# First batch in two parts of 256 and 320 queries, two buffers of turned P, one of x, and tile 1's scores beside P V

## The chip, the cores and the metric

The kernel runs on one core of a Trainium2 chip. A core has five engines that run side by side: TensorE (PE, matmuls, with its weight loads shown as PEld), VectorE (DVE), ScalarE (ACT), GpSimd (POOL) and SyncE (SP, which here only issues DMAs). Each engine takes its instructions strictly in the order in which they were written and waits at an instruction until its operands are there. The metric is the time of one execution on the device in microseconds (us); lower is better.

## The reference

Block-causal attention over 8 batches of 8 heads, 576 positions of 64 values each, followed by a feed-forward layer with three first matrices whose maximum is taken:

```python
# q, k, v: (8, 8, 576, 64) float32;  w1, w2, w3: (512, 768), w_out: (768, 512) float64
scores = scale * np.matmul(q, k.transpose(0, 1, 3, 2))
mask = block_i >= block_j                    # blocks of 64 positions
scores = np.where(mask, scores, -1000000000.0)
attn = np.exp(scores - np.max(scores, axis=-1, keepdims=True))
attn = attn / (np.sum(attn, axis=-1, keepdims=True) + 1e-09)
attn_out = np.matmul(attn, v)                # -> x: 4608 tokens of 512
h = np.maximum(np.maximum(x @ w1, x @ w2), x @ w3)
out = h @ w_out
```

## The kernel before

**Attention.** Two heads are a pair; a batch has four pairs, the program 32. Queries are cut into tiles of 128: tile t (0 to 3) needs the first 128(t+1) keys, and the last 64 queries of both heads make a tile 4 of their own over all 576 keys. A pair goes through these steps: load q, k and v (`load`, DMAs issued by SP); turn k and q on DVE (`turn_k`, `turn_q`, tile `kq`); scores on PE (`qk` in the groups (3,), (2,) and (1, 0), and `qk4`), into PSUM banks `sb`; scan for the maximum with the mask on DVE (`top`, `top4`, line 382); exponential on ACT (`exp`, line 445); sum and inverse on DVE; scale by the inverse on ACT or POOL (`scale`); turn P in 32 x 32 blocks on DVE into `pz` (`turn`, lines 470 and 474); move `pz` to `pt` by four DMAs for each head (`move`, line 480); and P V on PE (`pv`, line 651). The two halves of the result, 256 and 320 columns wide, are copied from PSUM to `x32`, and split into a high and a low part `xh`, `xl` (`out`, `x_high`, `x_low`).

**Weights.** The weights come as 64-bit numbers. A unit (class `Unit`, 24 of them: 18 of w1, w2, w3 and 6 of w_out) loads 512 KB and makes a high and a low part of it: `size` on ACT, five steps on DVE (`clamp`, `shift`, `sign`, `power`, `rest`), `high` on ACT, three matmuls on PE (`whole`, lines 325 to 327), `lower` on ACT. All 24 stand near the start of the program.

**Feed-forward.** A `Chunk` is one half (320 or 256 columns) of a batch: 18 products on PE (`product`, line 764, 12 matmuls each), the maximum on DVE (`most`, line 779), a high and a low part of h on ACT and POOL, and the projection (`project`, line 830). A chunk needs its half of all four pairs of its batch, and its weights.

**Order.** The code makes a list of jobs, each with costs by engine, a rank, the jobs that it follows and the buffers that it takes and gives. `in_order` plays the list through and writes down, engine by engine, the order in which the jobs begin; the program holds that order fixed. `rank` grows by `PAIR` for each pair; units get ranks `DELAY + PACE * u`. The numbers of buffers are in `slots`: one of `pz`, three of `x32`, one natural copy of q and k each.

Of the kernel before, what the change touches and what calls it, by code (L numbers as in the profile page):

```python
# [19 lines left out]
INF = 3.0e38  # L20
# [121 lines left out]
def kernel(  # L142
# [23 lines left out]
    DELAY = 60.0  # L166
    PACE = 3.0

    PAIR = 24
    TURN = 12  # L170
    NEAR = 2
    XB = 3
# [4 lines left out]
        x32_0=XB, x32_1=XB, xh0=4, xl0=4, xh1=4, xl1=4, m=2, osb=2, left=1, qn=1, kn=1,  # L177
        vn=2, kq=2, q8=2, pz=1, pt=3, rest=1,
# [59 lines left out]
    class Unit:  # L238


        def __init__(self, u, src, dst, n, prior, *early):
# [16 lines left out]
            for step, fast in (  # L258
                (self.clamp, True),
                (self.shift, True),  # L260
                (self.sign, False),
                (self.power, True),
                (self.rest, False),
            ):
                c = dve(512, fast)
                j = job({"DVE": c}, rank, step, after=(j,), take=("rest",) if step == self.rest else (), lasts=c + GAP)
            j = job({"ACT": act(512, False)}, rank, self.high, after=(j,))
            j = job({"PE": 6 * pe(512)}, rank, self.whole, after=(j,), take=("pm",), give=(*self.temps, "rest"))
# [47 lines left out]
        def rest(self, eng):  # L316
            self.c = moe.tile([P, 512], F32R, name="rest", bufs=1)
# [59 lines left out]
    )  # L377

    GROUPS = ((3,), (2,), (1, 0))
# [15 lines left out]
    class Head:  # L395
# [5 lines left out]
        def plan(self, t0):  # L401

            pair, exps = self.pair, {}
            for n, ts in enumerate(GROUPS):
                apart = None
                for t in ts:
# [3 lines left out]
                        t0 + n + 1,  # L410
# [3 lines left out]
                        take=("stat",) if n == 0 else (),  # L414
# [3 lines left out]
                    exps[t] = job({"ACT": act(m) + 185.0}, t0 + n + 2, self.exp, t, after=(d,), take=(f"p{t}",))  # L418
                join([exps[t] for t in ts], BANK)
            inv = job({"DVE": SMALL}, t0 + 5, self.sum, after=exps.values(), lasts=SMALL + GAP)  # L420
            inv = job({"DVE": SMALL}, t0 + 5, self.inverse, after=(inv,))
            scales = {
                t: job(norm_cost(P * (t + 1)), t0 + 7 + t / 2, self.scale, t, after=(inv,)) for t in range(4)
            }
            join(scales.values(), ("stat",))
            first = job({"DVE": dve(512) + dve(128)}, t0 + 11, self.turn, 4, after=(pair.scaled,), take=("pz",))
            self.turned = [first]
            for t in (3, 2, 1, 0):
                j = job({"DVE": dve(P * (t + 1))}, t0 + 12, self.turn, t, after=(scales[t], first))
                join((j,), (f"p{t}",))  # L430
                self.turned.append(j)
            self.moved = job(
                {"SP": 4 * SEND}, t0 + 13, self.move, after=self.turned, take=("pt",), give=("pz",), lasts=4 * SEND + TURNED
            )

        def top(self, eng, t):
# [3 lines left out]
            least(self.ps[t], mask[:, 512 - P * (t + 1) :], INF, self.stat[0][:, t : t + 1])  # L440

        def exp(self, eng, t):
            nm, sm, _ = self.stat
            self.p[t] = att.tile([P, P * (t + 1)], F32, name=f"p{t}", bufs=slots[f"p{t}"])
            nc.scalar.activation(  # L445
                self.p[t], self.ps.pop(t), AF.Exp, bias=nm[:, t : t + 1], scale=-1.0, accum_out=sm[:, t : t + 1]
            )

        def sum(self, eng):
            nc.vector.tensor_scalar_add(self.stat[2], self.stat[1], EPS)  # L450

        def inverse(self, eng):
            nc.vector.reciprocal(self.stat[2], self.stat[2])  # L453

        def scale(self, eng, t):
            normalise(eng, self.p[t], self.stat[2][:, t : t + 1])

        def turn(self, eng, t):

            if t == 4:  # L460
                self.pz = att.tile([P, 4 * (RUN + 16)], F32, name="pz", bufs=slots["pz"])
# [14 lines left out]
        def move(self, eng):  # L476
            self.pt = att.tile([P, 4, RUN], F32, name="pt", bufs=slots["pt"])
            z = self.pz.rearrange("p (j u) -> p j u", u=RUN + 16)
            for i in range(4):
                nc.sync.dma_start(self.pt[:, i], z[32 * i : 32 * i + 32, :, 0:RUN])  # L480
# [3 lines left out]
    class Pair:  # L484
# [3 lines left out]
        def __init__(self, b, hp):  # L488
            self.b, self.hp = b, hp
            self.heads = [Head(self, j) for j in range(2)]  # L490
            self.x32, self.o, self.xs, self.ps = [None, None], {}, {0: [], 1: []}, {}
            n = (b * NP + hp) % 2
            self.vn, self.q8 = vns[n].rearrange("p (c h d) -> p c h d", h=2, d=D), q8s[n]

        def plan(self, first):

            loads = {}
            for nm, n, r in (("kn", 4, -15), ("qn", 4, -15), ("vn", 3, -4)):
                loads[nm] = job({"SP": n * LOAD}, first + r, self.load, nm, take=(nm,), lasts=n * LOAD + DMA)
            r = first - TURN  # L500
            tk = job({"DVE": dve(512) + dve(64)}, r, self.turn_k, after=(loads["kn"],), take=("kq",), give=("kn",))
            tq = job({"DVE": dve(S)}, r + 1, self.turn_q, after=(loads["qn"], tk), give=("qn",))
            asked = job({"ACT": 2 * act(64, False)}, r + 2, self.ask, after=(tq,), take=("q8",))

            self.scored, prior = {}, None
            for n, ts in enumerate(GROUPS):
                prior = self.scored[ts] = job(
                    {"PE": 4 * pe(*[P * (t + 1) for t in ts], least=64) + 100.0},
                    first + n,
                    self.qk,  # L510
                    ts,
                    after=(tk, tq, prior),
                    take=2 * BANK,
                )
            tops, last = [], prior
# [16 lines left out]
            join((prior, last), ("kq",))  # L532
            join((last,), ("q8",))
            for j, h in enumerate(self.heads):
                h.plan(first + 4 * j)
            join([h.turned[0] for h in self.heads], ("p4",))

            moved = [h.moved for h in self.heads]
            prior, self.xjobs = None, {}
            for half in (1, 0):  # L540
                n, r = HALF[half], first + PAIR + 2 - half
                prior = job(
                    {"PE": 4 * pe(*[4 * (z - a) for _, a, z, *_ in PVT[half]], least=64) + 100.0},
                    r,
                    self.pv,
                    half,
                    after=(*moved, loads["vn"], prior),
                    take=("sb",),
                )
                done = job(  # L550
                    {"ACT": act(n), "DVE": dve(n)}, r + 2, self.out, half, after=(prior,), take=(f"x32_{half}",), give=("sb",)
# [6 lines left out]

        def load(self, eng, nm):
            src = {"qn": q, "kn": k, "vn": v}[nm]  # L560
            h0 = 2 * self.hp
            if nm != "vn":

                t = nats[nm].rearrange("p (b r) -> p b r", r=32)
                for i in range(4):
                    nc.sync.dma_start(  # L566
                        t[32 * i : 32 * i + 32],
                        src[self.b, h0 + i // 2, :, 32 * (i % 2) : 32 * (i % 2) + 32].rearrange(
# [3 lines left out]
                return  # L572
            for j in range(2):
                nc.sync.dma_start(
                    self.vn[:, 0:4, j, :], src[self.b, h0 + j, 0:512, :].rearrange("(c p) d -> p c d", p=P)
                )
            nc.sync.dma_start(self.vn[0:64, 4], src[self.b, h0 : h0 + 2, 512:S, :].rearrange("h p d -> p h d"))

        def turn_k(self, eng):
# [3 lines left out]
            src, dst = nats["kn"], self.k  # L583
# [328 lines left out]
```

## Time and profile before

| | us |
|---|---|
| median of 3 runs | 946.14 (945.66 to 950.25) |
| the profiled execution | 947.51 |
| its span, first to last instruction | 945.7 |
| mean granted TensorE clock | 0.976 of full |
| busy: PE, DVE, ACT, POOL | 899.5, 541.4, 449.2, 239.5 |

The span is what the trace divides; the time of the execution lies 1.8 us above it. Busy time counts an engine as busy while any of its instructions runs. A row of the timeline gives the start in us, the length in us, the engine, the line and operation, the tiles (out<-in) with the shape, the count of merged instructions, and in brackets the idle time ahead of it with what ended that. A row of the windows gives the stretch, its length, then for each engine its busy time with the count of instructions, the granted clock, the DMA share and GB/s. A matmul in 32-bit floats stands as two records in the trace.

### The profile page before, as it was taken

Reading aid. Unit: us, or ns where it says so; the run is one execution under the profiler, and the core shown is the slowest. Engines: PE = TensorE matmul, PEld = TensorE weight load, DVE = VectorE, ACT = ScalarE, POOL = GpSimd, SP = SyncE. Lnnn points to the kernel's source line nnn. Section 1 sums busy time; section 2 is a strip of 40 time slices with the busy share of each in tenths; the row PEclk is TensorE's granted clock in tenths of the full one; section 3 lists DMA queues with packets and bytes.
Section 4 is the critical chain, followed back from the end, with each engine's and each line's share of the span. In section 5 each row is a group of like instructions: output and inputs, shape, how many; then the busy total and the mean of one; then the engine's idle time right before and its main releaser. Section 6 shows DMA issues by size and latency. Waiting matters only on the chain.

```text
span 945.7 us, 16712 instructions
## 1 busy us (share of the span) xinstructions
PE 899.5 (95%) x5736; PEld 739.8 (78%) x5736; DVE 541.4 (57%) x1644; ACT 449.2 (47%) x1308; POOL 239.5 (25%) x363
## 2 busy tenths in 40 slices
PE   4776899999999999999999999999999999999998
PEld 2333577788878878888888888887888888898997
DVE  5899899766464737466464746465464646350111
ACT  5566566555454545345454545355345545332211
POOL 2233122223231222323231222223231223132201
PEclk9588799999999999999999999999999999999999
DMA  8977666655453544546453644545454533430010
GB/s 157 244 186 191 172 140 143 130 129 111 105 110 90 116 114 95 120 88 131 103 109 93 120 106 98 128 92 132 88 108 103 117 101 70 105 68 26 1 34 23
DMA packets 242516, 103.86 MB, mean 110 GB/s; under 512 B 195072, under 2 KB 237056, under 8 KB 242432
## 3 DMA queue, kind: packets, MB, share of 16 engines
q1 hardware_dynamic: 242432, 102.80, 48.6%
q8 instruction: 45, 0.74, 0.3%
q14 instruction: 39, 0.32, 0.1%
HBM read 40.89 MB, written 9.44 MB: 53 GB/s over the span
## 4 chain that ended last, share of the span: by engine, by line
PE 83%; DVE 6%; DMA 5%; SPq 3%; issue 1%; ACT 1%; DVEq 0%; ACTq 0%
PE pm L764 47%; PE pm L830 14%; PE sb L651 9%; PE sb L603 8%; DMA pt<-pz 3%; PE sb L609 3%; DVE pz L470 2%; SPq L480 1%; SPq L566 1%; PE pm L325 1%; DVE sb L382 1%; DMA w<-in_moe_w_dram 1%; DVE rest L318 0%; DMA wo<-in_moe_w_out_dram 0%; DVE wo L302 0%
## 5 line engine op out<-in xcount | busy, mean ns | idle before, releaser
L764 PE MATMUL pm<-xh,w 128*128 128x320 f32 (+1 forms) x2304 | 498.4, 303 | 0.0
L764 PEld LDWEIGHTS pm<-xh,w 128*128 128x128 f32 x2304 | 378.5, 190 | 34.9 <-issue 22.2
L764 PE MATMUL pm<-xl,w 128*128 128x256 f32 (+1 forms) x1152 | 340.8, 296 | 0.4 <-POOL xl L235 0.4
L764 PEld LDWEIGHTS pm<-xl,w 128*128 128x128 f32 x1152 | 218.5, 190 | 3.5 <-POOL xl L235 0.6
L382 DVE CUSTOM_DVE_ANT_0 sb<-sb,mask 128x384 f32<-128x384 f32 (+4 forms) x288 | 134.9, 507 | 141.4 <-PE sb L603 135.3
L445 ACT ACTIVATE p<-sb,nm 128x512 f32<-128x512 f32 (+3 forms) x256 | 133.6, 527 | 129.7 <-DVE nm L382 104.2
L470 DVE STREAM_TRANSPOSE pz<-p 128x512 f32<-128x512 f32 (+3 forms) x320 | 156.5, 526 | 62.5 <-DMA pt<-pz 38.5
L779 DVE TENSOR_TENSOR m<-pm,m 128x320 f32<-128x320 f32 (+1 forms) x192 | 85.5, 445 | 164.6 <-PE pm L764 164.4
L393 POOL TENSOR_TENSOR p<-p,rs 128x128 f32<-128x128 f32 (+4 forms) x143 | 102.5, 742 | 249.7 <-DVE rs L453 148.7
L235 POOL TENSOR_TENSOR hl<-m,hh 128x256 fp32r<-128x256 f32 x96 | 70.8, 737 | 291.6 <-ACT hh L230 256.8
L603 PE MATMUL sb<-kq 64*128 64x128 f32 (+3 forms) x512 | 102.6, 493 | 23.0 <-ACT p L445 11.3
L830 PE MATMUL pm<-wo,hh 128*128 128x512 f32 x384 | 118.8, 391 | 0.0
L651 PE MATMUL sb<-pt,vn 128*64 128x320 f32 (+4 forms) x896 | 104.7, 373 | 4.3 <-DMA pt<-pz 2.4
L230 ACT CAST hh<-m 128x256 fp32r<-128x256 f32 x96 | 38.8, 404 | 141.4 <-DVE m L779 141.3
L651 PEld LDWEIGHTS sb<-pt,vn 128*64 128x64 f32 x896 | 64.9, 141 | 45.9 <-issue 15.2
L235 POOL TENSOR_TENSOR xl<-x,xh 128x320 fp32r<-128x320 f32 (+1 forms) x64 | 51.4, 815 | 154.2 <-ACT xh L230 154.2
L603 PEld LDWEIGHTS sb<-kq 64*128 64x128 f32 x512 | 48.2, 196 | 50.6 <-issue 15.2
L391 ACT ACTIVATE p<-p,rs 128x384 f32<-128x384 f32 (+4 forms) x145 | 80.2, 604 | 8.4 <-DVE rs L453 4.5
L830 PEld LDWEIGHTS pm<-wo,hh 128*128 128x128 f32 x384 | 71.1, 188 | 14.4 <-issue 0.2
L830 PE MATMUL pm<-wo,hl 128*128 128x512 f32 x192 | 74.8, 389 | 0.0
L230 ACT COPY osb<-pm 128x512 f32<-128x512 f32 x36 | 21.2, 589 | 80.6 <-PE pm L830 77.0
L230 ACT COPY m<-pm 128x320 f32<-128x320 f32 (+1 forms) x96 | 38.1, 397 | 28.7 <-PE pm L764 16.1
(67 smaller groups left out, 707.0 us busy)
## 6 DMA issues: line engine op xcount, KB each, us to landing
pt<-pz SPq DMA_DIRECT2D x256, 200.0 KB, 3.7
kn<-in_k_dram SPq DMA_DIRECT2D x128, 72.0 KB, 2.4
qn<-in_q_dram SPq DMA_DIRECT2D x128, 72.0 KB, 2.4
w<-in_moe_w_dram SPq DMA_DIRECT2D x18, 512.0 KB, 5.2
vn<-in_v_dram SPq DMA_DIRECT2D x64, 128.0 KB, 2.6
out_dram<-osb SPq DMA_DIRECT2D x32, 256.0 KB, 2.2
wo<-in_moe_w_out_dram SPq DMA_DIRECT2D x6, 512.0 KB, 4.2
vn<-in_v_dram SPq DMA_DIRECT2D x32, 32.0 KB, 2.4
```

Of the source, the lines that this page charges most:

```text
L230: nc.scalar.copy(dst, src)
L235: {"DVE": nc.vector, "POOL": nc.gpsimd}[eng].tensor_tensor(out=dst, in0=a, in1=b, op=ALU.subtract)
L382: nc.vector.tensor_tensor_reduce(out=ps, in0=ps, in1=hidden, scale=-SCALE, scalar=first, op0=ALU.add, op1=ALU.min, accum_out=out_)
L391: nc.scalar.mul(p, p, r)
L393: nc.gpsimd.tensor_tensor(out=p, in0=p, in1=r.broadcast_to([P, p.shape[1]]), op=ALU.mult)
L445: nc.scalar.activation(self.p[t], self.ps.pop(t), AF.Exp, bias=nm[:, t : t + 1], scale=-1.0, accum_out=sm[:, t : t + 1])
L470: nc.vector.transpose(dst, p[:, 0 : n * P])
L603: nc.tensor.matmul(ps, self.q[h.own, P * t : P * (t + 1)], self.k[h.own, 0:w], start=True, stop=True)
L651: nc.tensor.matmul(o[h.own].rearrange("p (i u) -> p i u", u=n)[:, :, c0 : c0 + z - a], self.vn[:, kt, h.j, :], h.pt[:, :, a:z], start=(m = ...
L764: nc.tensor.matmul(self.ps, w[i, f][:, c, :], xx, start=(c == 0 and s == 0), stop=(c == NC - 1 and s == 2))
L779: nc.vector.tensor_tensor(out=m, in0=ps, in1=m, op=ALU.max)
L830: nc.tensor.matmul(self.po[: self.rows], h, w[f], start=(f == 0 and s == 0), stop=(f == NF - 1 and s == 2))
```

## The change

- The first batch is done as two sets of four pairs: `FRONT` (queries 0 to 255, tiles 1 and 0, keys 0 to 255) and `BACK` (queries 256 to 575, tiles 3, 2 and 4, all keys). After `FRONT` the chunk of batch 0's first 256 columns can begin, and the chunk of 320 columns after `BACK`. Keys and values of the first 256 positions are loaded and turned twice in that batch.
- From batch 1 on the score groups are (3,), (2, 0) and (1,), with (3,) and (2, 0) written as one job; in batches 2 to 7 tile 1's scores follow the P V of the pair before in one job (`both`).
- `pz` gets two buffers, `x32` one (of three). The natural copies of q and k hold two `FRONT` pairs side by side. The tile `rest` of a weight unit lives in the tile `left`.
- q of the first two batches is loaded by DMAs that ACT issues; SP issues the rest as before.
- Units have ranks from 16 in steps of 4 (before: from 60 in steps of 3).
- Sums and inverses are made once for the first groups and once for tile 1, so there are more of them.

```diff
-    DELAY = 60.0
-    PACE = 3.0
+    DELAY = 16.0
+    PACE = 4.0
     PAIR = 24
+    FRONT_PAIR = 8
+    BACK_PAIR = 20
+    SECOND = 9
-    XB = 3
+    XB = 1
...
-        x32_0=XB, x32_1=XB, xh0=4, xl0=4, xh1=4, xl1=4, m=2, osb=2, left=1, qn=1, kn=1,
-        vn=2, kq=2, q8=2, pz=1, pt=3, rest=1,
+        x32_0=XB, x32_1=XB, xh0=4, xl0=4, xh1=4, xl1=4, m=2, osb=2, left=1, qn=2, kn=2,
+        vn=2, kq=2, q8=2, pz=2, pt=3,
...
-    GROUPS = ((3,), (2,), (1, 0))
+    WHOLE = Part(((3,), (2, 0)), (1,), (1, 0), S, slice(0, S), slice(0, RUN), True)
+    EARLY = Part(((3,), (2, 0)), (1,), (1, 0), S, slice(0, S), slice(0, RUN))
+    FRONT = Part(((1, 0),), (), (0,), 256, slice(0, 256), slice(0, 96))
+    BACK = Part(((3,), (2,)), (), (1,), S, slice(256, S), slice(96, RUN))
...
+                e = "ACT" if nm == "qn" and not part.beside else "SP"
...
+            prior = job(
+                {"PE": sum(cost[ts] for ts in part.first) + 100.0},
+                first,
+                self.qk,
+                part.first,
+                after=(tk, tq, before and before.later),
+                take=2 * len(part.first) * BANK,
+            )
...
+            if part.beside:
+                self.later = job(
+                    {"PE": cost[part.later] + 200.0 + before.cost},
+                    first + SECOND,
+                    self.both,
+                    after=(prior, *pv),
+                    take=2 * BANK + ("sb", "sb"),
+                )
...
+        def both(self, eng):
+            self.prior.values(eng)
+            self.qk(eng, (self.part.later,))
...
+    front = plan(0, FRONT, FRONT_PAIR)
+    start = rank + SECOND + 6
+    back = plan(0, BACK, BACK_PAIR)
+    chunks.append((0, 0, front, start, rank + END))
+    start, pairs = rank + END, {0: back}
+    for b in range(1, B):
+        pairs[b] = plan(b, EARLY if b == 1 else WHOLE, PAIR)
+        if b == 1:
+            chunks.append((0, 1, back, start, rank + END))
```

How the instructions move, at three places. The first is PE near the start. `sb<-kq` are scores, `pm<-wo,plus` and the two rows after it are a weight unit, `sb<-pt,vn` is P V, `pm<-xh,w` are products. Before, the third pair's first scores, the first unit and the first P V:

```order
L603 MATMUL sb<-kq 128x512 x2
L603 MATMUL sb<-kq 128x384 x2
L325 MATMUL pm<-wo_233,plus 128x512
L326 MATMUL pm<-w_372,less 128x512
L327 MATMUL pm<-rest,plus 128x512
L651 MATMUL sb<-pt,vn_75 64x320 x6
L651 MATMUL sb<-pt,vn_75 64x4x48 x2
L651 MATMUL sb<-pt,vn_75 64x4x16 x2
L651 MATMUL sb<-pt,vn_75 64x256 x2
L651 MATMUL sb<-pt,vn_75 64x4x32 x2
```

After, the fourth `FRONT` pair's scores, the first P V (256 columns only), the second unit and the first products:

```order
L706 MATMUL sb<-kq 128x256 x2
L706 MATMUL sb<-kq 128x128 x2
L754 MATMUL sb<-pt,vn_75 64x256 x2
L754 MATMUL sb<-pt,vn_75 64x4x32 x2
L330 MATMUL pm<-wo_185,plus 128x512
L331 MATMUL pm<-w_304,less 128x512
L332 MATMUL pm<-left,plus 128x512
L867 MATMUL pm<-xh_333,w_251 128x256
L867 MATMUL pm<-xl_338,w_251 128x256
L867 MATMUL pm<-xh_333,w_251 128x256
```

Ahead of the 24th unit PE had all 216 products of 320 columns and none of 256; now it has all 216 of 256 columns, 57 of 320 and 15 of the projection.

The second is DVE at the last weight step (`rest` before, written to `left` now). Before, with rows of the seventh pair's turned k and q around it:

```order
L382 ISA nm 128x1
L296 TENSOR_SCALAR osb<-osb 128x512
L584 STREAM_TRANSPOSE kq<-kn 128x4x32x4
L585 STREAM_TRANSPOSE kq<-kn 128x16x4
L302 SCALAR_TENSOR_TENSOR osb<-wo_1502,osb 128x512
L634 SCALAR_TENSOR_TENSOR rs_1586<-sm_1585 128x1
L588 STREAM_TRANSPOSE kq<-qn 128x576
L779 TENSOR_TENSOR m<-pm,m 128x320
L308 TENSOR_SCALAR osb<-osb 128x512
L640 RECIPROCAL rs_1586<-rs_1586 128x1
L450 TENSOR_SCALAR rs<-sm 128x4
L318 SCALAR_TENSOR_TENSOR rest<-wo_1502,osb 128x512
```

After, among the turns of P of the first pair of batch 1:

```order
L510 STREAM_TRANSPOSE pz<-p_1627 128x4x4x32
L514 STREAM_TRANSPOSE pz<-p_1627 128x4x32
L510 STREAM_TRANSPOSE pz<-p_1483 128x4x4x32
L293 TENSOR_SCALAR osb<-osb 128x512
L510 STREAM_TRANSPOSE pz<-p_1491 128x3x4x32
L300 TENSOR_SCALAR osb<-osb 128x512
L510 STREAM_TRANSPOSE pz<-p_1504 128x4x32
L306 SCALAR_TENSOR_TENSOR osb<-wo_1527,osb 128x512
L510 STREAM_TRANSPOSE pz<-p_1555 128x2x4x32
L312 TENSOR_SCALAR osb<-osb 128x512
L882 TENSOR_TENSOR m<-pm,m 128x320
L323 SCALAR_TENSOR_TENSOR left<-wo_1527,osb 128x512
```

The last step stood at row 414 of DVE's order and now stands at row 374; the scans of seven pairs stood ahead of it, now those of five (`FRONT` and `BACK` together count as four).

The third is PE in a later batch. Before, the scores of tiles 1 and 0 stand among products, with the tile-4 scores `sb<-kq,q` close behind:

```order
L764 MATMUL pm<-xh_4355,w_895 128x320
L603 MATMUL sb<-kq 128x256 x2
L603 MATMUL sb<-kq 128x128 x2
L764 MATMUL pm<-xh_4775,w_895 128x320
L764 MATMUL pm<-xl_4785,w_895 128x320
L764 MATMUL pm<-xh_4775,w_895 128x320
L609 MATMUL sb<-kq,q_0_73 128x288 x2
```

After, tile 1's scores stand straight behind the P V of the pair before, here inside a projection:

```order
L933 MATMUL pm<-wo_1421,hl_5974 128x512
L754 MATMUL sb<-pt,vn_76 64x320 x6
L754 MATMUL sb<-pt,vn_76 64x4x48 x2
L754 MATMUL sb<-pt,vn_76 64x4x16 x2
L754 MATMUL sb<-pt,vn_76 64x256 x2
L754 MATMUL sb<-pt,vn_76 64x4x32 x2
L706 MATMUL sb<-kq 128x256 x2
L933 MATMUL pm<-wo_1462,hh_6023 128x512 x2
```

So a pair's last scores moved from a place of their own to the P V of another pair, and their P V follows at the next such place.

## Rows read from the trace of the kernel before

**Rows 1.** Windows: up to the last weight step on DVE, its unit, the rest.
```profile
0.00:173.30 173.30, 133.76 (x594) 83.70 (x594) 151.59 (x413) 105.24 (x284) 45.25 (x66) 0.87 0.72 174
173.30:177.70 4.40, 3.76 (x24) 2.38 (x26) 4.40 (x15) 4.20 (x10) 2.19 (x4) 1.00 0.63 103
177.70:942.30 764.60, 761.95 (x5120) 653.70 (x5120) 385.44 (x1220) 339.17 (x1015) 192.04 (x293) 1.00 0.44 96
```

**Rows 2.** Timelines of DVE and PE: last weight step; last matmul of unit 24.
```profile
173.35 0.68 DVE L318 SCALAR_TENSOR_TENSOR rest<-wo,osb 128x512 fp32r<-128x512 uint32 x1
...
177.30 0.40 PE L327 MATMUL pm<-rest,plus 128*128 128x512 f32 x1
```

**Rows 3.** Lines of DVE by form, 0 to 200 us (busy us, mean ns | idle before).
```profile
L470 DVE STREAM_TRANSPOSE pz<-p 128x512 f32<-128x512 f32 x30 | 21.0, 698 | 8.5 <-DMA pt<-pz 7.9
...
L584 DVE STREAM_TRANSPOSE kq<-kn 128x512 f32<-128x512 f32 x10 | 11.0, 1095 | 5.9 <-DMA kn<-in_k_dram 5.8
L382 DVE CUSTOM_DVE_ANT_0 sb<-sb,mask 128x512 f32<-128x512 f32 x16 | 10.9, 700 | 2.3 <-PE sb L603 2.3
...
L588 DVE STREAM_TRANSPOSE kq<-qn 128x576 f32<-128x576 f32 x10 | 7.7, 770 | 1.0 <-DMA qn<-in_q_dram 0.9
...
L779 DVE TENSOR_TENSOR m<-pm,m 128x320 f32<-128x320 f32 x12 | 5.6, 468 | 0.0
L382 DVE CUSTOM_DVE_ANT_0 sb<-sb,mask 128x128 f32<-128x128 f32 x16 | 4.6, 306 | 0.7 <-ACT p L445 0.7
...
L470 DVE STREAM_TRANSPOSE pz<-p 128x128 f32<-128x128 f32 x15 | 4.0, 269 | 0.0
```

**Rows 4.** Window of the first 20 us, columns as in rows 1.
```profile
0.00:20.00 20.00, 10.64 (x28) 5.79 (x29) 10.29 (x35) 10.27 (x32) 4.92 (x16) 1.00 0.78 156
```

**Rows 5.** Waits of DVE, 0 to 173.3 us (us in total, times, longest).
```profile
DVE pz L470 <- DMA pt<-pz: 2.6, 3, 1.4
```

**Rows 6.** Timeline of SP: q's first load; both heads' moves in a late batch.
```profile
2.79 2.12 SPq L566 DMA_DIRECT2D qn<-in_q_dram  x4
...
543.35 11.75 SPq L480 DMA_DIRECT2D pt<-pz  x8
```

**Rows 7.** Chain of waits: start, us, engine, line, count of records.
```profile
245.84 14.52 PE pm L764 x99
...
281.81 1.70 PE sb L603 x8
...
284.77 12.27 PE pm L830 x54
297.04 2.86 PE sb L651 x28
...
301.92 12.22 PE pm L764 x102
```

**Rows 8.** Timeline of PE: scores alone among products, and scores behind P V.
```profile
313.86 0.28 PE L764 MATMUL pm<-xh,w 128*128 128x256 f32 x1
314.07 1.13 PE L603 MATMUL sb<-kq 64*128 64x512 f32 x4
315.13 0.39 PE L764 MATMUL pm<-xh,w 128*128 128x256 f32 x1
315.36 0.28 PE L764 MATMUL pm<-xl,w 128*128 128x256 f32 x1
...
349.88 0.92 PE L603 MATMUL sb<-kq 64*128 64x256 f32 x8
350.73 0.41 PE L764 MATMUL pm<-xh,w 128*128 128x320 f32 x1
```

**Rows 9.** DMA issues on the page: count, KB each, us from issue to landing.
```profile
pt<-pz SPq DMA_DIRECT2D x256, 200.0 KB, 3.7
```

**Rows 10.** Timeline of PE: scores of one pair, and that pair's P V.
```profile
532.86 0.92 PE L603 MATMUL sb<-kq 64*128 64x256 f32 x8
...
558.42 3.26 PE L651 MATMUL sb<-pt,vn 128*64 128x320 f32 x28
```

More of the change, by code (lines that the diff above doesn't have):

```diff
@@ L399, in __init__, with plan @@
             self.ps, self.p = {}, {}
[L401 to L405, printed above, removed]
+        def plan(self, t0, after):
+            pair, part, scales, later = self.pair, self.pair.part, {}, []
+            for n, ts in enumerate(part.groups):
+                apart, exps, r = None, [], t0 + (SECOND if part.beside and ts == part.later else n)
                 for t in ts:
@@ L417, in plan @@
                         apart = job({}, 0, lambda eng: None, after=(d,), lasts=GAP)
[L418 to L424, printed above, removed]
@@ L425, in plan @@
-            join(scales.values(), ("stat",))
[L426 to L429, printed above, removed]
+                    exps.append(job({"ACT": act(m) + 185.0}, r + 2, self.exp, t, after=(d,), take=(f"p{t}",)))
+                join(exps, BANK)
+                later += exps
@@ new lines, in plan @@
+                later = []
+            join(scales.values(), ("stat",))
+            self.turned, first = [], None
+            if part.last:
+                first = job({"DVE": dve(512) + dve(128)}, t0 + 11, self.turn, 4, after=(pair.scaled, after), take=("pz",))
+                self.turned = [first]
+            for t in part.tiles:
+                j = job(
+                    {"DVE": dve(P * (t + 1))},
+                    t0 + 12,
+                    self.turn,
+                    t,
+                    after=(scales[t], first or after),
+                    take=() if first else ("pz",),
+                )
+                first = first or j
@@ L434, in plan @@
             )
+            return first
         def top(self, eng, t):
@@ L498, in plan @@
+        def plan(self, first, before):
+            part, loads = self.part, {}
             for nm, n, r in (("kn", 4, -15), ("qn", 4, -15), ("vn", 3, -4)):
-                loads[nm] = job({"SP": n * LOAD}, first + r, self.load, nm, take=(nm,), lasts=n * LOAD + DMA)
+                e = "ACT" if nm == "qn" and not part.beside else "SP"
+                took = (nm,) * (part.loads if nm != "vn" else 1)
+                prior = before and before.loads[nm]
+                loads[nm] = job({e: n * LOAD}, first + r, self.load, nm, after=(prior,), take=took, lasts=n * LOAD + DMA)
@@ L500, in plan @@
             r = first - TURN
[L501 to L513, printed above, removed]
-                )
@@ L515, in plan @@
-            tops, last = [], prior
+            n = part.queries.stop - part.queries.start
+            tk = job({"DVE": dve(part.keys)}, r, self.turn_k, after=(loads["kn"],), take=("kq",), give=("kn",) * part.loads)
+            tq = job({"DVE": dve(n)}, r + 1, self.turn_q, after=(loads["qn"], tk), give=("qn",) * part.loads)
+            cost = {ts: 4 * pe(*[P * (t + 1) for t in ts], least=64) for ts in part.groups}
+            prior = job(
[6 more added lines that the diff above has]
+            )
@@ new lines, in plan @@
+            last = prior
+            if part.last:
+                last = self.plan4(first, tq, prior)
+            join((self.later if part.later else prior, last), ("kq",))
+            turn = before and before.heads[1].first
+            for j, h in enumerate(self.heads):
+                turn = h.plan(first + 4 * j, turn)
+            if part.last:
+                join([h.turned[0] for h in self.heads], ("p4",))
+            self.loads = loads
+            self.cost = 4 * pe(*[4 * (z - a) for h in part.halves for _, a, z, *_ in PVT[h]], least=64)
@@ L516, in plan, with plan4 @@
+        def plan4(self, first, tq, last):
+            asked = job({"ACT": 2 * act(64, False)}, first - TURN + 2, self.ask, after=(tq,), take=("q8",))
+            tops = []
             for a in range(2):
```

193 lines of the change are left out of this document (120 added, 73 removed).

## The prediction

> **What bounds the kernel now.** I read the windows first, then the timelines where two of them meet. From 177.7 us to the last matmul at 942.3 PE is busy for 762.0 of 764.6 us at full clock, while DVE is busy for half of it [rows 1]: that stretch is as long as PE's work. Ahead of it the engine that hardly rests is DVE, 151.6 of 173.3 us, where PE's records cover 133.8 at a mean clock of 0.87 [rows 1]. The border is the last weight unit: its last DVE step begins at 173.35 and its last matmul on PE stands at 177.30 [rows 2]. So the time is a sum of three: DVE's busy time up to the last weight step (151.6) and its idle time there (21.7), the 4.4 us from that step to the end of the unit on PE, and what PE's order holds behind it (764.6). The last 3.4 us of the span and the 1.8 us outside it I leave as they are.
>
> How idle PE is ahead of the border can be told by price. Back to back at full clock a product of 320 columns takes 14.52/99 = 0.147 us, one of 256 12.22/102 = 0.120, a projection matmul 12.27/54 = 0.227, a pair's P V 2.86 [rows 7]. At such prices the work that PE's order holds ahead of the border comes to about 109 us, in 177.7. DVE is what PE waits for; making PE's early work cheaper gains nothing, and bringing the last weight step forward gains one for one.
>
> **Term 1: DVE's work ahead of the last weight step.** The change gives PE chunk work for 256 columns early, so fewer attention steps stand ahead of the 24 units. Counting DVE's order up to the last step, before against after, at the means of [rows 3], other widths on a line by columns between two rows: scans of two pairs fewer (four each of 512, 384, 256 and 128 columns at 0.700, 0.57, 0.44 and 0.306, and four of 288 at 0.47), -9.9; turns of P, six of 512 fewer at 0.698, three of 384, three of 256 and six of 128 at 0.555, 0.41 and 0.269, -8.7; turned k, two whole ones fewer at 1.095 with their ends and four half-width ones more at about 0.55, -0.5; turned q, six of 576 fewer at 0.770, four of 256 and four of 320 more, -1.5; maxima, nine of 320 fewer at 0.468, twelve of 256 more at about 0.41, +0.7; four copies of x at about 0.43 and some 13 small sums and inverses at about 0.12 more, +3.3. The sum is -16.6. Records of neighbours overlap: the whole list before adds to about 187 at such means, where the window has 151.6 busy, so -16.6 counts for -13.5. Between the two I take -14, nearer to the scaled one: 137.6.
>
> **Term 2: DVE's idle time ahead of it.** Of the 21.7 us, 9.7 fall in the first 20 us [rows 4], while the first pair's data arrive and go round PE and ACT once. q's first load is issued after k's, 2.1 us later [rows 6], and now starts beside it on ACT; the first scores are narrower. Against that a FRONT pair gives DVE a third of a pair's work to fill the same waits. I let the two cancel; each alone is bounded by some 3 us. The three waits for the single buffer of turned P, 2.6 us [rows 5], end with two buffers: 19.1. The rest I leave, but here lies the largest unknown. Below: the q loads that SP no longer issues are 2.1 us of its queue each [rows 6], twelve of them, and all loads and moves behind them come earlier; that could take away half of the remaining waits, -9. Above: those 2.1 us now stand in ACT's own order, 12 x 2.1 = 25 us on an engine that was busy for 105.2 + 4.2 of 177.7 us [rows 1]. What waits behind an issue there are exponentials and weight casts, and DVE waits for both. ACT would come to about 135 of 161 us less two pairs' exponentials, so it is not the bound, but a third of these issues reaching DVE would be +8. The last step then begins at 137.6 + 19.1 = 156.7 (148 to 165), and the unit ends on PE at 161.1 instead of 177.7: **-16.6**.
>
> That the FRONT moves are short weighs on the same term. A move of 96 columns has a quarter of the bytes of one of 400; in proportion to its bytes it lands 0.9 us after its issue instead of 3.7 [rows 9]. The Trainium skill (DMA: Bandwidth & Descriptors, Specifications) asks for 512 bytes or more in a piece for full rate and says that below it the engine reads, modifies and writes; 96 numbers of 4 bytes are 384. By that rule a front move would take as long as a whole one, the first chunk would start some 3 us later, and the sum would come to 930 instead of 927; no row before has a piece of that size in a move.
>
> **Term 3: PE's work behind the unit.** By PE's order 159 products of 320 columns more (+23.3), 216 of 256 fewer (-25.9), 15 projections fewer (-3.4), and attention for about two pairs more (scores of four heads, two P V halves of 320 and one of 256), +10.0 without its switches: **+4.0**. The switches are the gain of the joined jobs. Scores of 512 keys for both heads are 512 columns in four passes at 2.4 GHz, 0.853 us, but start to start they take 1.06, the step into them 0.21 and out of them 0.23 where two products stand 0.12 apart [rows 8]: 0.2 within and 0.2 around. Two score groups joined, 512 and 384, take 1.70 for 1.49 of columns [rows 7], so they pay that once. Scores behind P V take 0.85 for 0.64 [rows 8], so this kind of join saves only the 0.2 around. Counting PE's order behind the unit, kinds in a row go from 95 to 81 and islands among products from 83 to 56: 14 x 0.2 + 27 x 0.2 = **-8.2**. One buffer of x costs nothing as long as a pair's x is split before the next P V, which stands 15 us or more behind; sums and inverses of tile 1 apart are DVE work in a stretch where DVE is half idle. For tile 1's later place (first rival) I add **+2**; below nothing, above some 36.
>
> **Sum.** -16.6 + 4.0 - 8.2 + 2 = -18.8 us. The profiled execution took 947.51, 1.4 above the median of 946.14; I take the difference off the median: **927 us**. Behind the border PE should not starve: the sixth pair's P is turned about 16 us of DVE work behind the last step, at 173, and moved by 181, and PE comes to that P V after 27 us of other work, at 188.
>
> **Rivals.**
>
> *Slower: the joined job waits.* In batches 2 to 7 PE reaches the P V of a pair inside `both`, and all of PE's order stands behind it. Before, 25.6 us lay between a pair's last scores and its P V [rows 10]. After, two of the four such gaps in a batch hold only 12 projections, one group of joined scores, 66 products and the tile-4 scores, or 87 products and the same scores: 15.5 and 15.8 us. In that time tile 1 must be scanned, exponentiated, summed, scaled and turned for both heads, with the next pair's k and q among it on DVE (some 5 us), eight moves must be issued, at 0.6 us each 4.8 (the eight of [rows 6] take 11.75, but with the wait for the one buffer among them), and the last must land, 3.7 [rows 9]: 13.5. The 2 us to spare speak against it; that a row like the 3.26 of [rows 10] is already 0.4 longer than 2.86 speaks for it. At 12 tight places it eats the gain if each waits 1.7 us; at 3 us, with the allowance of 2 in it, the time is 927 + 34 = 961. Chance 0.09.
>
> *No change: the last weight step comes no earlier.* DVE's work shrinks but the waits grow by as much, ACT's issues being the likeliest cause, or the moves of FRONT, which share SP's queue with the weight loads. Then only term 3 is left: 942 to 946. Chance 0.11.
>
> *Faster still: DVE's waits shrink too.* SP's queue was issuing nearly without a break at the start and loses the q loads; idle falls from 19 to 10, and the last step begins at 148: 918. With the allowance for the joined job unused, DVE's work down by the full 16.6 and the 3 us of the start gained as well it would be 910. Chance 0.17.
>
> **The numbers.** The forecast of 927 has 0.63; its own range is 918 to 938. For 8 in 10 I take 910 to 944: the lower end is the third rival's extreme, the upper leaves out the slower one and the top of the unchanged. Half a per cent, 4.7 us, is about what a measurement of this kernel can tell from no change. Faster by over that is the forecast with the third rival, 0.80; within it the second, 0.11; slower the first, 0.09.
>
> **What would show it.** The last weight step on DVE at 157, its unit off PE at 161, with DVE busy for about 138 us ahead of it; PE busy without a break for about 762 us behind; no wait of DVE's turns for a move; P V of 2.86 with scores right behind them, without idle time before. Wrong it would be made by P V records that wait at the two tight places of a batch, by ACT rows whose idle time ends at its own DMA issues with DVE waiting for exponentials, or by a last weight step at 165 or later.

## The result and the profile after

The changed kernel takes 934.0 us (median of 4 runs, 932.1 to 934.6) where the kernel before, measured beside it, took 945.9: a ratio of 0.986, 95% interval 0.983 to 0.989. That is 12 us or 1.4%, clear of no change; the forecast was 19 us, 927. The profiled executions took 947.51 and 933.72, 13.8 apart.

The windows, cut where [rows 1] were cut (last weight step on DVE, end of its unit on PE, last matmul):

```profile
0.00:159.00 159.00, 121.14 (x594) 77.60 (x595) 135.38 (x374) 87.80 (x221) 40.74 (x59) 0.95 0.69 169
159.00:162.30 3.30, 3.30 (x18) 2.49 (x17) 3.19 (x9) 0.94 (x2) 0.00 (x0) 1.00 0.84 156
162.30:928.60 766.30, 761.54 (x5129) 655.01 (x5127) 422.31 (x1388) 368.75 (x1092) 205.39 (x309) 1.00 0.45 101
...
0.00:20.00 20.00, 5.80 (x25) 4.05 (x26) 9.92 (x41) 6.97 (x22) 4.11 (x17) 1.00 0.62 133
```

The two rows that set the border, from the timelines of DVE and PE, as in [rows 2]:

```profile
158.96 0.68 DVE L323 SCALAR_TENSOR_TENSOR left<-wo,osb 128x512 fp32r<-128x512 uint32 x1
...
161.91 0.39 PE L332 MATMUL pm<-left,plus 128*128 128x512 f32 x1
```

The unit is off PE at 162.3 instead of 177.7: 15.4 us earlier, 16.6 were forecast. But PE then needs 766.3 us instead of 764.6 [rows 1], where the forecast had it 2.2 us shorter. So most of what is missing was lost behind the border, in the stretch in which PE was to run without a break.

Of PE's waits there the view names only 4.4 us (the line, what it waited for, us in total, times, longest):

```profile
PE sb L754 <- issue: 1.6, 2, 1.1
PE sb L754 <- DMA pt<-pz: 1.0, 2, 0.8
PE pm L867 <- POOL xl L239: 0.8, 1, 0.8
PE sb L712 <- ACT p L485: 0.8, 2, 0.5
PE pm L867 <- ACT wo L234: 0.2, 1, 0.2
```

The larger part hides in busy time. In an undisturbed P V the two heads' records begin in pairs, 0.007 us apart at 470 us. Where the second head's data is late, the first head's first two records run early and alone and the other 26 start later; these two cover 0.75 us by themselves, so a delay of up to about 0.7 us shows no idle time. No record is stretched: the longest is 0.483 us in the P V at 450 us as in the undisturbed one at 470. PE's timeline at one of the tight places (a score group behind P V, then the P V of the pair whose scores these were), and another in the next batches:

```profile
433.44 0.70 PE L706 MATMUL sb<-kq 64*128 64x256 f32 x4
...
449.77 0.75 PE L754 MATMUL sb<-pt,vn 128*64 128x320 f32 x2
450.72 2.89 PE L754 MATMUL sb<-pt,vn 128*64 128x320 f32 x26 [0.19 <-DMA pt<-pz]
...
657.79 0.75 PE L754 MATMUL sb<-pt,vn 128*64 128x320 f32 x2
659.62 2.89 PE L754 MATMUL sb<-pt,vn 128*64 128x320 f32 x26 [1.08 <-issue]
```

From the first record to the start of what follows, these two take 3.77 and 4.66 us instead of the 2.86 of [rows 7], though the view counts 0.19 and 1.08 as idle. Measured so, seven P V behind the border are long, at 241, 348, 450, 556, 658, 679 and 766 us, by 0.74 to 1.80 us each and 7.7 in all; six of them are the first tight place of a batch. The kernel before had seven such, 6.3 us in all (the 3.26 of [rows 10] is the smallest but one).

What a P V at 450 waits for is read from SP's timeline and from the chain of waits. SP:

```profile
438.62 1.98 SPq L662 DMA_DIRECT2D kn<-in_k_dram  x4
440.70 6.58 SPq L520 DMA_DIRECT2D pt<-pz  x8
447.32 3.04 SPq L662 DMA_DIRECT2D qn<-in_q_dram  x4
```

The chain:

```profile
444.13 0.23 SPq L520
...
444.40 1.20 SPq L520
...
445.65 0.60 SPq L520
...
446.29 4.29 DMA pt<-pz
450.58 0.14 issue
450.72 2.89 PE sb L754 x22
```

Tile 1's scores end at 434.1 and the last move lands at 450.6: 16.4 us, for which the forecast had 13.5. The four moves of the first head stand behind the next pair's k load on SP until 440.7, those of the second are issued up to 447.3, and the last takes 4.3 us to land.

### The profile page after: what moved, and what is told of

The parts are those of the page before. It is cut to its first block, busy times and chain, and to the rows that moved or that the text cites. A ratio compares the mean times of both kernels' runs of the same rounds, so it can differ in the third digit from the quotient of the medians.

```text
span 931.9 us, 17031 instructions
## 1 busy us (share of the span) xinstructions
PE 886.0 (95%) x5736; PEld 735.1 (79%) x5736; DVE 560.9 (60%) x1768; ACT 457.9 (49%) x1315; POOL 246.1 (26%) x368
## 4 chain that ended last, share of the span: by engine, by line
PE 77%; DVE 10%; DMA 6%; issue 2%; ACT 2%; SPq 1%; POOL 0%; DVEq 0%; ACTq 0%
PE pm L867 44%; PE pm L933 15%; PE sb L754 8%; PE sb L706 7%; PE sb L712 2%; DMA w<-in_moe_w_dram 2%; DVE pz L510 2%; DMA qn<-in_q_dram 2%; DVE sb L405 2%; ACT p L485 1%; DMA pt<-pz 1%; DMA kn<-in_k_dram 1%; DVE left L323 1%; SPq L520 1%; DVE kq L683 1%
## 5 line engine op out<-in xcount | busy, mean ns | idle before, releaser
L867 PE MATMUL pm<-xh,w 128*128 128x320 f32 (+1 forms) x2304 | 491.2, 302 | 2.5 <-ACT xh L234 1.6
L882 DVE TENSOR_TENSOR m<-pm,m 128x256 f32<-128x256 f32 (+1 forms) x192 | 86.3, 449 | 165.2 <-PE pm L867 164.5
L510 DVE STREAM_TRANSPOSE pz<-p 128x384 f32<-128x384 f32 (+3 forms) x320 | 159.6, 528 | 37.6 <-ACT p L414 17.7
L485 ACT ACTIVATE p<-sb,nm 128x256 f32<-128x256 f32 (+3 forms) x256 | 134.3, 527 | 93.6 <-DVE nm L405 75.9
L416 POOL TENSOR_TENSOR p<-p,rs 128x128 f32<-128x128 f32 (+4 forms) x148 | 108.3, 751 | 244.1 <-DVE rs L493 168.7
L933 PE MATMUL pm<-wo,hh 128*128 128x512 f32 x384 | 123.8, 403 | 0.4 <-ACT wo L234 0.4
L706 PE MATMUL sb<-kq 64*128 64x384 f32 (+3 forms) x512 | 91.8, 478 | 16.7 <-DVE kq L690 16.7
L414 ACT ACTIVATE p<-p,rs 128x256 f32<-128x256 f32 (+4 forms) x140 | 82.3, 603 | 24.1 <-DVE rs L493 17.7
L933 PEld LDWEIGHTS pm<-wo,hh 128*128 128x128 f32 x384 | 70.5, 188 | 18.2 <-issue 1.7
L234 ACT COPY m<-pm 128x256 f32<-128x256 f32 (+1 forms) x96 | 38.1, 397 | 33.2 <-PE pm L867 21.7
L485 ACT ACTIVATION_READ_ACCUMULATOR p<-sb,nm 128x1 f32 x256 | 50.3, 196 | 0.0
```

What stands on the lines that cost most here:

```text
L234: nc.scalar.copy(dst, src)
L414: nc.scalar.mul(p, p, r)
L416: nc.gpsimd.tensor_tensor(out=p, in0=p, in1=r.broadcast_to([P, p.shape[1]]), op=ALU.mult)
L485: nc.scalar.activation(self.p[t], self.ps.pop(t), AF.Exp, bias=nm[:, c : c + 1], scale=-1.0, accum_out=sm[:, c : c + 1])
L510: nc.vector.transpose(dst, p[:, 0 : n * P])
L706: nc.tensor.matmul(ps, self.q[h.own, P * t : P * (t + 1)], self.k[h.own, 0:w], start=True, stop=True)
```

## The experiments

Each run is compared with the kernel before measured beside it (its median there was 947.4 to 948.2); the ratio to it is the number that compares from run to run, and the changed kernel's is 0.986. Gaps of PE work between tile 1's scores and P V are worked out from PE's order at the prices of [rows 7] and counted from the start of the scores; from their end, as the prediction counted, they are 0.6 to 0.7 less.

### Which of the joins is worth what: four corners

The scores are joined in two ways. Early (`BACK`, batch 1): (3,) and (2,), or (3,) and (2, 0), are one job. Late (batches 2 to 7): this, and tile 1 behind P V. Four kernels with each undone or kept.

Without any join:

```diff
-            prior = job(
-                {"PE": sum(cost[ts] for ts in part.first) + 100.0},
-                first,
-                self.qk,
-                part.first,
-                after=(tk, tq, before and before.later),
-                take=2 * len(part.first) * BANK,
-            )
+            self.scored, prior = {}, before and before.later
+            for n, ts in enumerate(part.first):
+                prior = job({"PE": cost[ts] + 100.0}, first + n, self.qk, (ts,), after=(tk, tq, prior), take=2 * BANK)
+                self.scored[ts] = prior
...
-    WHOLE = Part(((3,), (2, 0)), (1,), (1, 0), S, slice(0, S), slice(0, RUN), True)
+    WHOLE = Part(((3,), (2, 0)), (1,), (1, 0), S, slice(0, S), slice(0, RUN))
```

(and q of batches 2 to 7 stays on SP by `self.b < 2`.)

> As the run before, and the scores of (3,) and (2, 0) are two jobs again, each with its place, in every batch: no score group is joined with anything. PE's order has 28 islands and 32 changes of kind more behind the last weight unit than the changed kernel. Theory of the forecast, 0.2 us each: 12 us more, 946. Theory A, by the trace of the changed kernel, where 14 kinds and 27 islands fewer were worth about 5.5 us instead of 8.2 (0.13 each): 8 us more, less up to 4 of waits that go, so 938 to 942. If the joins are worth nothing: 934.

Measured: 933.89, ratio 0.9852 (0.9836 to 0.9868). The same as with all joins, so all of them together were worth nothing.

Early undone, late kept: the same loop for parts that are not `beside`, one job for the others.

```diff
+            for n, groups in enumerate([(ts,) for ts in part.first] if not part.beside else [part.first]):
```

> One edit to the changed kernel (934.0): the scores of BACK and of batch 1 are asked for group by group again, not (3,) and (2, 0) in one job; batches 2 to 7 keep both joins. Theory A (the early join holds up the start: it wants twice the banks at once, and the run without any join had 7.9 us less idle time of PE ahead of 200 us): the start as in that run, the last unit off PE near 148 with 84 us of work ahead of it; PE's order 2.6 us longer than the changed kernel's; 927, between 925 and 930. Theory B (that start came from the late groups too, or what it saves is waited for later): 933 to 937.

Measured: 928.55, ratio 0.9791 (0.9772 to 0.9809). The last weight step begins at 145.5, its unit is off PE at 149.4.

Early kept, late undone: the loop with `if self.b > 1`, `WHOLE` not `beside`, and q of batches 2 to 7 on SP.

> The other corner: BACK and batch 1 keep (3,) and (2, 0) in one job, batches 2 to 7 have no join (three places for scores, P V alone). Start as in the changed kernel, last unit off PE at 161 to 162. PE's order is 11 us longer. Theory A (joins in the late batches save PE 0.2 us for each change, less about 3 us of P V waits that go with the roomier order): 940 to 943. Theory B (the late joins are worth nothing, as the equal times of the run without joins and the changed kernel would suggest): 933 to 936.

Measured: 940.06, ratio 0.9913 (0.9898 to 0.9928).

So by the ratios the late joins gain 0.0061 (early undone) or 0.0053 (early kept) and the early ones lose 0.0069 (late kept) or 0.0061 (late undone): some 5 to 6.5 us each way, and the two effects add. The loss is read from the window of the first 150 us, in this order: the changed kernel, late undone, early undone, no joins.

```profile
0.00:150.00 150.00, 112.66 (x547) 71.30 (x548) 127.80 (x356) 84.01 (x211) 40.13 (x58) 0.94 0.70 175
```

```profile
0.00:150.00 150.00, 114.48 (x553) 71.52 (x554) 129.28 (x358) 83.88 (x211) 40.24 (x59) 0.94 0.71 175
```

```profile
0.00:150.00 150.00, 116.50 (x569) 74.07 (x570) 133.41 (x375) 88.21 (x223) 40.40 (x58) 0.95 0.71 177
```

```profile
0.00:150.00 150.00, 120.64 (x575) 76.76 (x576) 133.73 (x379) 88.86 (x224) 40.60 (x58) 0.93 0.72 178
```

DVE, which bounds this stretch, idles for 22.2 and 20.7 us with the early join and for 16.6 and 16.3 without. The gain of the late joins is PE's: its busy time over the whole program is 885.98 in the changed kernel and 895.04 with them undone, for 55 switches, 0.16 each; by the other pair (885.25 and 895.69, for 56) it is 0.19. (A switch is an island, a place where scores or P V stand among other matmuls, or a change of kind within one; as in the prediction's count, the tile-4 scores are left out.) These are low: busy time also holds the hidden part of the P V waits behind the border, 5.1 us against 2.6 in the first pair and 6.2 against 3.4 in the other, and without it the prices are about 0.21 and 0.24. Not all of that reaches the time, since the late joins also bring the longer waits. That a joined job must find twice the banks of scores free at once is the likely reason why it comes later at the start; that was not tried.

### Tile 1 apart, the rest joined

```diff
-    WHOLE = Part(((3,), (2, 0)), (1,), (1, 0), S, slice(0, S), slice(0, RUN), True)
+    WHOLE = Part(((3,), (2, 0)), (1,), (1, 0), S, slice(0, S), slice(0, RUN))
```

(q of batches 2 to 7 stays on SP here too.)

> Undone: tile 1's scores behind P V in batches 2 to 7 (they get a place of their own again, P V too); the split of batch 0, the two buffers of turned P and the joined job of (3,) and (2, 0) stay. The changed kernel took 934.0. By its trace PE's time behind the last weight unit grew by 2.1 us instead of falling by 2.2. Theory A (the join saves switches but its P V waits at one place in a batch, five waits of 0.3 to 1.4 us, 4.1 in all): PE's order is 2.4 us longer at 0.2 a switch and the waits go, so 932.3, between 931 and 934. Theory B (the forecast's: the waits are small beside what the join saves, and would be there without it): 936 to 940. The part ahead of the last weight step is the same in both, 159.

Measured: 938.48, ratio 0.9914 (0.9892 to 0.9935): 5 us slower than the changed kernel. The time is theory B's, and theory A falls in the form in which it was put: the waits don't belong to the join. They are still there, since the new order has places with only 14.4 us of work between tile 1's scores and P V. And the time is that of the run with both late joins undone (0.9913): alone, the joined job of (3,) and (2, 0) gave nothing measurable in the late batches, so the late gain came with tile 1 behind P V, by itself or together with that job; the one without the other was not tried. PE's timeline at one:

```profile
363.44 0.75 PE L754 MATMUL sb<-pt,vn 128*64 128x320 f32 x2
365.63 2.24 PE L754 MATMUL sb<-pt,vn 128*64 128x320 f32 x18 [1.44 <-DMA pt<-pz]
```

### Room at the tight places

If the waits belong to the order's tightness, the planner must only be told that moves land later in batches 2 to 7:

```diff
-                {"SP": 4 * SEND}, t0 + 13, self.move, after=self.turned, take=("pt",), give=("pz",), lasts=4 * SEND + TURNED
+                {"SP": 4 * SEND}, t0 + 13, self.move, after=self.turned, take=("pt",), give=("pz",), lasts=4 * SEND + TURNED + (2500.0 if part.beside else 0.0)
```

In the changed kernel, alone:

> One number of the changed kernel (934.0): the planner counts 2.5 us more for the landing of the moves of batches 2 to 7; (3,) and (2, 0) stay joined everywhere. In the changed kernel seven P V behind the last weight unit take 3.6 to 4.7 us instead of 2.86, 7.7 in all, six of them the first P V of a batch with 16.1 us of work ahead of it. Theory A (those waits are the tight places'): they go, and nothing else changes: 926 to 928. Theory B (what the room gave depends on the start without the join): 931 or more.

Measured: 925.04, ratio 0.9762 (0.9746 to 0.9777): 0.0098 or 9 us, for one number. With the same work behind the border as the changed kernel, PE needs 7.9 us less there, and P V makes up 7.7 of it:

```profile
160.90:919.30 758.40, 756.49 (x5128) 651.32 (x5127) 423.84 (x1392) 363.69 (x1081) 208.80 (x315) 1.00 0.46 102
```

With early groups apart as well:

> As the run before, and the planner counts 2.5 us more for the landing of the moves of batches 2 to 7, so that 18.2 to 18.7 us of PE work instead of 16.1 to 16.5 lie between tile 1's scores and that pair's P V at the two tight places of a batch; work and buffers are the same. Theory A (the P V waits of 0.3 to 1.4 us at those places come from the tightness): they go, 3 to 4 us less than the run before, 923 to 926. Theory B (the waits come from something else, a queue or DVE's order): the same time as the run before within 1 us.

(The run before is here the one with early groups apart, 928.55.)

Measured: 920.63, ratio 0.971 (0.9691 to 0.973), the fastest of all. Of PE's records behind the last unit those of P V alone became shorter: from start to start all of them take 772.9 us in that run and 765.0 here, and the 7.9 us between stand in P V. From 218 us on each takes 2.86; one row of PE's timeline, with the 0.07 by which it overlaps the record that follows:

```profile
445.11 2.93 PE L756 MATMUL sb<-pt,vn 128*64 128x320 f32 x28
```

18.2 us of work ahead of P V (17.5 from the scores' end) are enough and 16.1 (15.5) are not, which fits the 16.4 us from there to the landing. I had expected 3 to 4 us from the idle time that the views name; it was twice that, which fits the hidden part.

### The second buffer of turned P

```diff
-        vn=2, kq=2, q8=2, pz=2, pt=3,
+        vn=2, kq=2, q8=2, pz=1, pt=3,
```

> Undone: the second buffer of turned P, alone. The planner then writes another order, in which a pair's last scores stand 19 us or more of PE work ahead of its P V everywhere from batch 2 on (16.1 at the tight places of the changed kernel). Theory A: ahead of the last weight step DVE waits for moves again, 2.6 us as before or some more, and the step moves from 159 to 162 to 166; behind it the P V waits at the tight places (4.1 us) go; 933 to 937 in all. Theory B (the second buffer carries the gain at the start): last step at 170 or later, 943 or more.

Measured: 941.84, ratio 0.9932 (0.9917 to 0.9948). The buffer is worth 7 to 8 us, but neither theory had the place. The last weight step begins at 147.7, not later. The time is lost behind the border, about half of it at the passage to the joined batches, where PE is busy for 4 us less and one P V, at 223 us, takes 8.1 us; the window of 200 to 300 us, the changed kernel and this one:

```profile
200.00:300.00 100.00, 98.38 (x633) 81.07 (x633) 68.13 (x232) 57.26 (x175) 31.30 (x48) 1.00 0.59 132
```

```profile
200.00:300.00 100.00, 94.33 (x587) 78.54 (x586) 57.43 (x188) 45.77 (x143) 26.87 (x38) 0.98 0.55 118
```

The same edit in the fastest kernel:

> The fastest run so far (920.6) with one buffer of turned P. In the changed kernel, with tight places and early joins, the second buffer was worth 7.8 us (941.8 without). Theory A (the buffer is worth a lot at the start, where turns wait for moves): 927 to 932. Theory B (most of those 7.8 us came from the early joins and the tight order that met it, and a roomy order needs no second buffer): 920 to 924.

Measured: 1018.57, ratio 1.0754 (1.0733 to 1.0774), far from both. With one buffer and moves that last longer the planner writes an order with 24 to 28 us of work ahead of three P V of a batch and 10 to 12 ahead of the fourth. There PE stands still; its timeline at one:

```profile
694.59 1.30 PE L756 MATMUL sb<-pt,vn 128*64 128x320 f32 x2 [2.62 <-DMA pt<-pz]
703.29 5.02 PE L756 MATMUL sb<-pt,vn 128*64 128x320 f32 x26 [7.40 <-DMA pt<-pz]
```

Seven P V, the one at 226 us and one in each later batch, take 11.3 to 14.3 us, together 74 more than seven of 2.86. The buffer can't be valued apart from the order that is written for it.

### q loads by SP

```diff
-                e = "ACT" if nm == "qn" and not part.beside else "SP"
+                e = "SP"
```

> Undone: ACT's issue of the q loads in the first two batches; SP issues all of them again. Theory A (ACT has room, SP's queue has none at the start): the last weight step comes later by some part of the 12 x 2.1 us that SP issues again, 2 to 8 us; 936 to 942. Theory B (ACT's issues, 22 us of its order, hold up exponentials and casts): earlier by up to 4 us, 930 to 933. Behind the border nothing changes.

Measured: 935.4, ratio 0.9865 (0.9848 to 0.9883), no difference. The last weight step begins at 159.2 as in the changed kernel. What ACT's issues give is seen in the first window only, DVE 9.92 us busy with them (above) and 7.96 without; by the border it is gone:

```profile
0.00:20.00 20.00, 3.69 (x18) 2.75 (x20) 7.96 (x34) 7.46 (x25) 3.28 (x14) 1.00 0.48 92
0.00:159.20 159.20, 115.86 (x578) 75.86 (x579) 135.81 (x371) 89.88 (x231) 39.39 (x53) 0.92 0.70 169
```

### The split and the ranks of the units

The split undone, with one buffer of turned P and the old ranks:

```diff
-    front = plan(0, FRONT, FRONT_PAIR)
-    start = rank + SECOND + 6
-    back = plan(0, BACK, BACK_PAIR)
-    chunks.append((0, 0, front, start, rank + END))
-    start, pairs = rank + END, {0: back}
+    pairs = {0: plan(0, EARLY, PAIR)}
+    start = rank + END
...
```

> Undone: the split of batch 0 (batch 0 like batch 1, both chunks behind it), with the ranks of the weight units as before (60, step 3) and, since this has no room for more, one buffer of turned P and a tile of its own for rest; the joins, one x buffer and q on ACT stay. To be compared with the run with one buffer (941.8), which has the split. Theory A (the split brings the start forward): last unit off PE at 172 or later, 946 to 950. Theory B (the time is won by the joins alone, the split only moves work about): 939 to 943.

Measured: 937.36, ratio 0.9885 (0.9867 to 0.9903): 4 us faster than the split with one buffer (0.9932), nearest to theory B and below its range. The pair differs in the ranks of the units as well as in the split. The split undone in the fastest kernel, with two buffers and the early ranks:

> The fastest run so far (room at the tight places, early scores group by group; 920.6) with the split of batch 0 undone: batch 0 like batch 1, both of its chunks behind it, two buffers of turned P and the ranks of the units kept, and the last 64 positions of the first chunk split only when all weights are there. PE's order is 1.6 us shorter. Theory A (the split carries the start, PE has chunk work while DVE makes weights and turns): PE idles until batch 0 is through, and the time is 930 to 940. Theory B (the split is worth nothing, since DVE is the bound of the start and does the same work either way, as the pair of runs with one buffer suggests, 941.8 with it and 937.4 without): 918 to 923.

Measured: 941.74, ratio 0.9937 (0.9923 to 0.9951): 21 us slower than with the split, above theory A's range. Two windows of the fastest kernel, then of this one:

```profile
20.00:60.00 40.00, 29.50 (x95) 13.10 (x93) 36.89 (x113) 24.44 (x65) 10.09 (x14) 0.91 0.68 161
60.00:100.00 40.00, 36.52 (x206) 26.68 (x207) 36.86 (x86) 25.19 (x56) 10.82 (x11) 0.91 0.87 247
```

```profile
20.00:60.00 40.00, 26.51 (x77) 12.60 (x77) 34.40 (x100) 20.63 (x51) 8.08 (x9) 0.71 0.82 221
60.00:100.00 40.00, 30.17 (x103) 14.90 (x105) 33.03 (x94) 25.18 (x62) 6.98 (x8) 0.78 0.63 172
```

PE has 180 records here instead of 301, at a mean granted clock of 0.71 and 0.78 of 2.4 GHz instead of 0.91 (1.2 GHz is its other level), and DVE too does less. So the two pairs of runs disagree in sign, and what the split is worth alone stays open. With units early, two buffers and room it was worth 21 us, likely because the units then stand ahead of attention and only a chunk that can begin gives PE work. Split and early units together cost 4 us with one buffer; no run has the split with late units and one buffer.

The fastest kernel with other ranks of the units:

```diff
-    DELAY = 16.0
-    PACE = 4.0
+    DELAY = 30.0
+    PACE = 3.0
```

> The fastest run so far (920.6) with the weight units at ranks from 30 in steps of 3 instead of from 16 in steps of 4; the last unit keeps nearly its rank (99 for 108). Theory A (what counts is DVE's total work ahead of the last weight step and PE's work behind it, and an order only moves between the two): 918 to 924. Theory B (early units let the first chunk begin early, and PE idles longer without them): 925 to 930.

Measured: 923.37, ratio 0.9741 (0.9722 to 0.976). The last unit is off PE at 161.4 instead of 150.2 and the time is 3 us more: theory A's, as the border moves by 11 us and nearly all of it is work that changes sides.

## Why the prediction came out as it did

The time fell inside the forecast's own range, 918 to 938, but not by its sum: the third term came out with the other sign.

**The bound** held: DVE ahead of the last weight step, PE behind it.

**Term 1** was right. DVE is busy for 135.4 us ahead of the last step; 137.6 were forecast. That these 2.2 us made up for half of the next term's miss is luck.

**Term 2** was 4.5 us short: idle time is 23.6 us instead of 19.1. The first 20 us (10.1 idle against 9.7) came out nearly as put, and q on ACT neither helped nor harmed. The move waits of the turns [rows 5] were to end with two buffers; 1.4 of the 2.6 us are still there. What was not priced is the joined job at the start: with groups apart DVE idles for 5.6 us less in the first 150. The step begins at 159.0 instead of 156.7, and since the unit then leaves PE 3.3 us later, not 4.4, the border is 1.2 us late.

**Term 3** was mis-sized, and holds most of the error: -2.2 were forecast, +1.7 measured. The work of +4.0 was counted from PE's order. The allowance of 2 us for waits was too small: long P V went from 6.3 to 7.7 us, and 1.8 us of waits at 163 to 212 us are new, +3.2. Without their waits the two stretches are 764.6 - 6.3 = 758.3 and 766.3 - 7.7 - 1.8 = 756.8 us; with 4.0 more work in the second, the switches saved 5.5 us, not 8.2: 0.13 for each of the 41 counted. The run with room alone gives the same, 758.4 - 1.9 = 756.5 us without waits. The four corners give 0.2 or a little more for a switch, so they don't show that the price was too high. The count may be what is off: it leaves out the tile-4 scores, which behind the border stand at 38 places in PE's records before and at 47 after; that this is the cause is not shown. Underneath lies one slip in the first rival: the chain from tile 1's scores to the landed move was put at 13.5 us and takes 16.4, because the next pair's k load stands ahead of the moves on SP, the eight issues span 6.6 us instead of 4.8 and the last lands in 4.3 us. The room of 15.5 to 15.8 us was not enough, and P V that waits at the tight places is what the prediction had named first as a sign of being wrong.

**The rivals.** The slower one is at work, at one of the two tight places of a batch (once at the other) instead of both and with 1.1 us each instead of 3; the order with 10 to 12 us of room shows it at full size. The faster one's last weight step (148) is about that of the kernels with the early groups apart and the ranks kept (145.5 and 146.4), but not by its mechanism: DVE still idles for 16.5 and 17.1 us there instead of 10, and the rest is some 6 us of DVE's work that now stands behind the step (129.0 and 129.3 us busy ahead of it). Its time is reached only with room as well, 920.6. "No change" did not come, and its likeliest cause, ACT's issues, is refuted by the run with q on SP.

**Pieces under 512 bytes.** The moves of `FRONT` land 2.1 us after their issue (the median; single ones took 1.9 to 4.7), those of `BACK`, also ahead of the border, in 3.2:

```profile
pt<-pz SPq DMA_DIRECT2D x32, 152.0 KB, 3.2
pt<-pz SPq DMA_DIRECT2D x32, 48.0 KB, 2.1
```

A whole move takes 3.9 over the program. So neither the 0.9 in proportion to the bytes nor the 3.7 of the other reading, which was the prediction's own inference, came out: by the medians, 1.8 us less for 152 KB less, on a part of some 1.5 us that does not shrink. The three kinds ran beside different traffic, so this is an estimate. The Trainium skill (DMA: Bandwidth & Descriptors, Anatomy of one DMA) states such a fixed part, about 2 us, for DMAs that GpSimd issues; these were issued by SP, so the two agree in kind only. A penalty for 384-byte pieces is not to be seen.

## What to carry to other kernels

Fewer switches on the bounding engine are a gain only where that engine bounds: tile 1's scores behind P V gave 5 to 6 us in the stretch that PE bounds, while two score groups in one job cost 6 to 6.5 at the start, where others wait for the results. When an order is fixed ahead of time, measure the whole chain from a producer to its late consumer, queue neighbours included, and compare it with the work placed between; two microseconds too few at one place in each batch were worth 9 us here. A planner's constant that is too low is found from the time between the consumer's first record and what follows it, not from its idle time.

## What was not expected of the hardware

A late operand shows little as idle time of PE: for 7.7 us of long P V the waits view has 2.6 us, since the first two records of the head that is not late run ahead alone, and their 0.75 us count as busy. Eight moves issued one behind the other took SP 6.6 us in the late batches, four at the start 2.5.
